# Attention into a two-stage MoE: value products with queries on partitions, row sums from a column of ones

## The chip, the cores and the metric

One Trainium2 chip; the kernel runs on one of its cores. A core has five instruction streams: PE (TensorE, matmuls, with its weight loads shown apart as PEld), DVE (VectorE), ACT (ScalarE), POOL (GpSimd) and SP (SyncE, which here only issues DMAs). Each stream runs its own instructions in the order in which they stand in the program and waits on semaphores for the others. The metric is the device time of one execution in microseconds (us), the median of several runs.

## The reference

Three stages follow each other. The first is an attention with local and global tokens (4 batches, 8 heads, 512 local and 32 global tokens, head size 64); the second a dense layer pair with a piecewise activation; the third a routed layer pair with eight experts. Only the first is touched here:

```python
k_all = concat([k_g, k_l]);  v_all = concat([v_g, v_l])        # 32 + 512 tokens
out_g = sm(scale * q_g @ k_all.T) @ v_all                      # every global query sees all 544
s_ll = where(abs(i - j) <= 32, scale * q_l @ k_l.T, -1e9)      # a local query sees a band of 65 ...
a_l = sm(concat([scale * q_l @ k_g.T, s_ll]))                  # ... and the 32 global tokens
out_l = a_l @ concat([v_g, v_l])
# sm(s): e = exp(s - max(s));  e / (sum(e) + 1e-9)
```

## The kernel before

The attention is cut into 8 units (4 batches, 2 groups of 4 heads). A unit has two head pairs (`hl` = 0, 1), and a head pair has two steps of 2 x 128 queries, so a unit has four steps `k` = 0 to 3. A step works on `i` = 0 to 3: two query tiles by two heads.

What a unit does, with the names of its tiles:

- `pair`, `tr_k`, `tr_q`: keys and queries of a head pair are copied side by side (`kp`, `qp`), transposed on PE into `pk`, `pq` and copied to `kw`, `qT`. `kw` holds for every 64 queries 64 local keys and the 32 global keys (a block of 96 columns), so that 160 columns from a block's start hold the 128 local keys of a window and the global ones, with the window cut in two. `kw_g` writes the global keys into the blocks.
- `scores` (L484): PE forms `s`, 160 scores for each query; DVE (L496) adds the mask and takes the row's extreme into `st`; ACT (L506) takes the exponential into `sm` and has the row sum added up on the way, which it reads out with an instruction of its own (ACTIVATION_READ_ACCUMULATOR).
- `fin`: DVE turns the sums into reciprocals (L523, L524), POOL multiplies the rows by them (`pn`, L528, four of them; `smg`, L532, the global columns).
- `trans`: PE transposes `pn` into `ta` (four) and `smg` into `tb`; ACT copies them to `ptA` and `ptB`.
- `pval`: PE forms the output transposed, head dimension on partitions, in `pv`: the values are the weights (`va`, `vb` for the two halves of a window, L580; `vgz` for the global tokens, L593), the probabilities stream through. `ptA` has 32 more columns for each tile, which hold the global queries' probabilities (`pglob`), so that the global output falls out of the same matmuls (and of two more, L586). ACT copies `pv` to `xs`; `gsum` sums the global part into `xg` and stores the local part to DRAM (`xsc`) from ACT's DMA queue.
- `glob_s` to `glob_t`: scores `sg` of the global queries (L424, L421), maximum, exponential with sums, division on POOL (L455), transposition into `pgT`.

Between these stand pieces that prepare the weights of the second stage (`conv_half` on DVE, `conv_parts` on ACT and POOL). Two pieces of the second stage's first matmul (`up1`, tile `hps`) are put into the attention's last unit; `act1`, `down1` (tile `yp`) follow.

The order of all this is written out by hand: every call gets a number from the table `AT` (a unit is 16 long, so unit `n` starts at 16 n; the names with `z_` are those of unit 0), the calls are sorted by it, and each engine's stream follows. PSUM, where matmuls write, is held in pools: `psh` with two buffers for `s` and `hps`, and `ps` with three buffers under the tag T (`ta`, `tb`, `sg`) and three under the tag y (`pk`, `pq`, `pgt`, `pv`).

Of the kernel before, what the change touches and what calls it, by code (L numbers as in the profile page):

```python
# [22 lines left out]
    scores=[-0.929, 3.577, 6.9, 12.21], fin=[6.425, 8.774, 10.199, 17.022],  # L23
    trans=[9.521, 10.799, 15.847, 20.797], pglob=[9.927, 14.287, 19.392, 22.324],
    pval=[13.081, 18.61, 24.832, 25.923], gsum=[27.805, 30.229], glob_s=1.311, glob_m=2.56, glob_e=3.521,
    glob_n=4.146, glob_p=6.373, glob_t=9.066, ld0=-3.002, ld1=-0.136, ld_v=18.09, ld_vb=15.197, ld_vg=16.913,
    k0=9.379, q0=10.782, k1=14.997, q1=14.811, u0=127.057, u1=141.542, rk0=3.621, rq0=4.32, rk1=9.51,
    rq1=11.797, e_k='V', e_q='V', e_g='P', bp=1, e_kc='A', e_kd='A', e_w='V', e_fl='P', e_qc='A', f4='PPPP',
    e_p='P', e_ta='A', e_tb='A', e_xs='A', e_pt='V', e_pu='V', gl=6.839, gt0=22.889, gt1=24.82,
    z_scores=[0.0, 1.0, 5.699, 12.227], z_fin=[2.374, 7.66, 10.375, 14.481],  # L30
    z_trans=[3.713, 13.16, 15.237, 21.686], z_pglob=[8.77, 15.092, 19.345, 23.598],
    z_pval=[14.413, 19.634, 23.697, 26.493], z_glob_s=2.772, z_glob_m=3.337, z_glob_e=3.472, z_glob_n=3.787,
    z_glob_p=5.475, z_glob_t=7.797, cl=[17.691, 30.997, 37.177, 47.387, 52.623, 67.27, 78.231, 90.2, 98.587],
    xh=[25.339, 28.196, 38.872, 43.513, 47.597, 59.508, 67.7, 73.729],
    xlo=[25.905, 33.595, 42.625, 46.625, 54.263, 70.623, 75.965, 79.01], cp=1.664,
)
CV = [1.668, 10.165, 12.547]
# [4 lines left out]
def kernel(  # L42
# [88 lines left out]
    ps = at_st.enter_context(tc.tile_pool(name="ps", bufs=3, space=PSUM))  # L131
# [3 lines left out]

    HP = P // 2
    NW = P + G
    BW = HP + G
# [149 lines left out]
    NH = 4  # L288
# [12 lines left out]
    def ld_va(n):  # L301
        u = units[n]
        u.va = ap_.tile([P, NH, NT, D], F32, name="va", tag="va", bufs=2)
        r0 = (u.b * H + NH * u.g) * S - W
        vat = u.va.rearrange("p h t d -> p (h t) d")
# [7 lines left out]
    def ld_vb(n):  # L313
        u = units[n]
        u.vb = ap_.tile([P, NH, NT, D], F32, name="vb", tag="vb", bufs=2)
        r0 = (u.b * H + NH * u.g) * S + W
        vbt = u.vb.rearrange("p h t d -> p (h t) d")
# [6 lines left out]
    def ld_vg(n):  # L324
# [3 lines left out]
        for j in range(2):  # L328
            for t in range(2):
                p0 = (2 * t + j) * G  # L330
                nc.sync.dma_start(
                    out=vz[p0 : p0 + G, :, t, j * D : (j + 1) * D],
                    in_=v_g[u.b, h0 : h0 + NH].rearrange("(l j) s d -> j s l d", j=2)[j],
                )
        nc.sync.dma_start(out=u.vb[HP + W :, :, NT - 1], in_=v_g[u.b, h0 : h0 + NH].rearrange("h s d -> s h d"))

    class Unit:
        def __init__(self, n):
# [5 lines left out]
            self.pn = {}  # L344
            self.xs = {}
            self.st = {}
            self.pt = {}
            self.ptA = {}
# [3 lines left out]
    NKW = 8 * BW + HP  # L352
# [14 lines left out]
    def tr_k(n, hl):  # L367
        u = units[n]
        pk = ps.tile([P, S], F32, name="pk", tag="y")
# [3 lines left out]
        copy(  # L373
            AT["e_kc"],
            kw[:, BW : 8 * BW].rearrange("p (c x) -> p c x", x=BW)[:, :, :HP].rearrange("p c (y t) -> p c y t", t=NT),
            pk.rearrange("p (t y) -> p y t", t=NT)[:, 8 : P - 8, :].rearrange("p (c y) t -> p c y t", c=7),
        )
        copy(
            AT["e_kd"],
            kw.rearrange("p (c x) -> p c x", x=W)[:, 1 : NKW // W - 1 : NKW // W - 3, :].rearrange(  # L380
                "p c (y t) -> p c y t", t=NT
            ),
            pk.rearrange("p (t y) -> p y t", t=NT).rearrange("p (c y) t -> p c y t", c=16)[:, 0:16:15],
        )
# [3 lines left out]
    def kw_g(n, hl):  # L388
# [5 lines left out]
            kw[:, : 8 * BW].rearrange("p (c x) -> p c x", x=BW)[:, :, HP:],  # L394
            kg.unsqueeze(1).to_broadcast([P, 8, G]),
# [3 lines left out]
            kw.rearrange("p (c x) -> p c x", x=W)[:, 0 : NKW // W : NKW // W - 1, :],  # L399
# [3 lines left out]
    def tr_q(n, hl):  # L403
        u = units[n]
        pq = ps.tile([P, S], F32, name="pq", tag="y")
# [5 lines left out]
    def glob_s(n):  # L411
        u = units[n]
        sg = ps.tile([P, 512], F32, name="sg", tag="T")
        sg2 = ps.tile([P, 512], F32, name="sg2", tag="y")
        for glob in range(2):
            for i in range(2):
                for j in range(2):
                    rs = slice((2 * i + j) * G, (2 * i + j + 1) * G)
                    lq = qgz[:, 2 * u.g + i, j, u.b * G : (u.b + 1) * G]
                    if glob:  # L420
                        nc.tensor.matmul(sg2[rs, :G], lhsT=lq, rhs=u.kw[i][:, HP:BW], start=True, stop=True)  # L421
                        continue
                    kl = u.kw[i][:, W : W + 8 * BW].rearrange("p (c y x) -> p c y x", c=8, x=W)[:, :, 0:3:2, :]
# [3 lines left out]
    def glob_m(n):  # L427
# [3 lines left out]
        nc.vector.tensor_reduce(out=m[:, 0:1], in_=sg, axis=AX.X, op=ALU.max)  # L431
        nc.vector.tensor_reduce(out=m[:, 1:2], in_=sg2[:, :G], axis=AX.X, op=ALU.max)
# [4 lines left out]
    def glob_e(n):  # L437
# [3 lines left out]
        pl, pr = pg[:, W : W + S], pg[:, W + S :]  # L441
        nc.scalar.activation(out=pl, in_=sg, func=AF.Exp, scale=scale, bias=m[:, 2:3], accum_out=m[:, 3:4])
        nc.scalar.activation(out=pr, in_=sg2[:, :G], func=AF.Exp, scale=scale, bias=m[:, 2:3], accum_out=m[:, 4:5])

    def glob_n(n):
        u = units[n]
        m = u.gm
        nc.vector.tensor_scalar(
            out=m[:, 5:6], in0=m[:, 3:4], scalar1=m[:, 4:5], scalar2=1e-9, op0=ALU.add, op1=ALU.add
        )  # L450
        nc.vector.reciprocal(out=m[:, 6:7], in_=m[:, 5:6])

    def glob_p(n):
        m = units[n].gm
        nc.gpsimd.tensor_scalar(  # L455
            out=pg[:, W:], in0=pg[:, W:], scalar1=m[:, 6:7], scalar2=1.0, op0=ALU.mult, op1=ALU.mult
        )

    def glob_t(n):
# [3 lines left out]
        pt = ps.tile([P, NT, P], F32, name="pgt", tag="y")  # L463
# [7 lines left out]

    def scores(n, k):
# [3 lines left out]
        st = u.st[k] = ap_.tile([P, 3, 4], F32, name="st", tag="st", bufs=4)  # L476
        sj = [psh.tile([P, 2, NW], F32, name=f"s{j}", tag="h") for j in range(2)]
        for tt in range(2):
            t = 2 * uu + tt
            for j in range(2):  # L480
                for c in range(2):
                    q0 = t * P + c * HP
                    k0 = (2 * t + c) * BW
# [7 lines left out]
        for j in range(2):  # L491
            for tt in range(2):
# [11 lines left out]
                    accum_out=st[:, 0, i : i + 1],  # L504
# [10 lines left out]
    def sel(x):  # L515

        ap = x[:, :HP]
        return bass.AP(ap.tensor, ap.offset, [list(ap.ap[0]), [BW, 2], [1, HP]])

    def fin(n, k):  # L520
        u = units[n]
        sm, st = u.sm.pop(k), u.st.pop(k)
        nc.vector.tensor_scalar(out=st[:, 2, :], in0=st[:, 1, :], scalar1=1e-9, scalar2=None, op0=ALU.add)  # L523
# [1104 lines left out]
```

## Time and profile before

| what | us |
|---|---|
| median of 3 runs (lowest, highest) | 747.02 (746.94, 748.74) |
| the profiled execution, its own time | 748.24 |
| its span in the trace | 746.5 |
| attention, until `yp` starts | 146.5 of it |

The profiled execution lies 1.22 us above the median of the runs. Its span is 1.74 us shorter than its device time; what lies around the span is not in the trace. A row of the timeline gives the start, the duration, the engine, the line, the operation and the tiles; where matmuls follow one another, the distance between two starts is the cost, since a matmul's shown end overlaps the next start. Matmuls stand twice in the trace when both operands are fp32 and it isn't a transposition: "x4" are then two matmuls of the program. The granted clock of TensorE was 1.00 of full speed in all of the attention.

### The profile page before, as it was taken

The page shows a single profiled execution, that of the slowest core. Times are in us where ns is not written, and L with a number is a line of the kernel's source. Part 1 is how long each engine was busy: PE and PEld are TensorE (multiplying, and loading weights), DVE is VectorE, ACT ScalarE, POOL GpSimd, SP SyncE. Part 2 cuts the span into 40 slices and gives each one's busy share as a digit, 9 for nine tenths or more (in the row PEclk, how much of TensorE's full clock was granted, in tenths as well). Part 3 has the DMA queues.
Part 4 walks back from the last instruction along what each step waited for, and adds up shares of the span by engine and source line. Part 5 has one row for each costly group of instructions (what it writes and reads, how often), then busy time and mean ns, then how long its engine had stood idle before and what let it go on. Part 6 is the DMA issues. An engine that isn't in the chain of part 4 may idle for free.

```text
span 746.5 us, 14099 instructions
## 1 busy us (share of the span) xinstructions
PE 734.2 (98%) x4999; PEld 592.5 (79%) x4999; DVE 480.7 (64%) x1473; ACT 372.2 (50%) x929; POOL 138.2 (19%) x301
## 2 busy tenths in 40 slices
PE   8999999999999999999999999999999999999996
PEld 6776776788888888888898888888888876777774
DVE  4899997388888757777698866785788322211111
ACT  4899998655455565455556646555312212211111
POOL 4676776312111100000000100000003002001011
PEclk9999999999999999999999999999999999999999
DMA  8678884423343612000200032212301466557560
GB/s 191 161 196 219 227 207 123 115 86 114 113 124 103 225 58 72 0 1 1 98 1 1 1 98 71 72 35 93 100 0 57 148 230 226 179 192 269 174 228 25
DMA packets 83067, 86.45 MB, mean 116 GB/s; under 512 B 42816, under 2 KB 57152, under 8 KB 82992
## 3 DMA queue, kind: packets, MB, share of 16 engines
q1 hardware_dynamic: 75760, 77.64, 34.9%
q0 software_dynamic: 1648, 4.98, 1.7%
q10 hardware_dynamic: 5584, 2.88, 1.4%
q8 instruction: 41, 0.67, 0.4%
q14 instruction: 34, 0.28, 0.1%
HBM read 73.93 MB, written 11.94 MB: 115 GB/s over the span
## 4 chain that ended last, share of the span: by engine, by line
PE 77%; issue 13%; DMA 4%; DVE 2%; ACT 2%; POOL 2%; POOLq 0%; ACTq 0%
PE yp L881 25%; PE hps L832 25%; PE eh L1359 7%; PE eo L1381 6%; DMA out<-ob,ide 3%; PE s L484 3%; PE pv L580 3%; PE pv L593 2%; PE ta L552 1%; POOL out L1393 1%; PE wt L1471 1%; PE sg L424 1%; PE pq L407 1%; DVE sm L496 1%; PE pk L371 1%
## 5 line engine op out<-in xcount | busy, mean ns | idle before, releaser
L832 PE MATMUL hps<-xh,winh 128*128 128x512 f32 (+2 forms) x320 | 115.0, 359 | 0.0
L832 PE MATMUL hps<-xl,winh 128*128 128x512 f32 (+2 forms) x320 | 114.4, 358 | 0.0
L832 PE MATMUL hps<-xh,winl 128*128 128x512 f32 (+2 forms) x320 | 114.3, 357 | 0.0
L881 PE MATMUL yp<-woh,gh 128*128 128x512 f32 x272 | 107.5, 395 | 0.4 <-ACT gh L850 0.4
L881 PE MATMUL yp<-wol,gh 128*128 128x512 f32 x272 | 106.3, 391 | 0.0
L1365 DVE SCALAR_TENSOR_TENSOR el<-eh,eg 128x512 fp32r<-128x512 f32 (+2 forms) x40 | 24.4, 611 | 100.1 <-ACT eg L1364 99.8
L1364 ACT ACTIVATE eg<-eh 128x512 fp32r<-128x512 f32 (+2 forms) x40 | 21.4, 535 | 105.9 <-PE eh L1359 102.6
L832 PEld LDWEIGHTS hps<-xh,winh 128*128 128x128 f32 x320 | 60.3, 188 | 9.0 <-PE pv L593 0.2
L832 PEld LDWEIGHTS hps<-xh,winl 128*128 128x128 f32 x320 | 60.3, 188 | 8.5
L832 PEld LDWEIGHTS hps<-xl,winh 128*128 128x128 f32 x320 | 60.2, 188 | 7.6
L1393 POOL DMA_INDIRECT out<-ob,ide x17 | 17.1, 1006 | 249.3 <-DVE ob L1390 245.7
L1359 PE MATMUL eh<-exh,wh 128*128 128x512 f32 (+2 forms) x160 | 59.6, 372 | 0.0
L881 PEld LDWEIGHTS yp<-woh,gh 128*128 128x128 f32 x272 | 51.1, 188 | 10.2 <-ACT gh L850 0.8
L881 PEld LDWEIGHTS yp<-wol,gh 128*128 128x128 f32 x272 | 51.2, 188 | 9.4
L1359 PE MATMUL eh<-exl,wh 128*128 128x512 f32 (+2 forms) x160 | 57.3, 358 | 1.0 <-PEq L1569 1.0
L1359 PE MATMUL eh<-exh,wl 128*128 128x512 f32 (+2 forms) x160 | 57.2, 358 | 0.0
L506 ACT ACTIVATE sm<-sm,st 128x160 f32<-128x160 f32 x128 | 53.4, 427 | 4.9 <-DVE st L496 4.9
L1381 PE MATMUL eo<-wh,eg 128*128 128x512 f32 x136 | 53.3, 392 | 0.0
L1381 PE MATMUL eo<-wh,el 128*128 128x512 f32 x136 | 53.1, 391 | 0.0
L1381 PE MATMUL eo<-wl,eg 128*128 128x512 f32 x136 | 53.1, 391 | 0.0
L528 POOL TENSOR_SCALAR pn<-sm,st 128x128 f32<-128x128 f32 x128 | 50.7, 416 | 9.0 <-DVE st L524 4.4
L865 DVE TENSOR_TENSOR wol<-wof,woh 128x512 fp32r<-128x512 f32 x64 | 43.9, 686 | 0.0
(808 smaller groups left out, 1590.6 us busy)
## 6 DMA issues: line engine op xcount, KB each, us to landing
rw<-in_moe_w SPq DMA_DIRECT2D x64, 256.0 KB, 4.4
rw<-in_moe_w SPq DMA_DIRECT2D x24, 512.0 KB, 4.8
raw<-in_moe_w_out SPq DMA_DIRECT2D x12, 512.0 KB, 3.7
raw<-in_moe_w_in SPq DMA_DIRECT2D x11, 512.0 KB, 3.7
k<-in_k_l SPq DMA_DIRECT2D x16, 256.0 KB, 3.0
ysc<-y SPq DMA_DIRECT2D x16, 256.0 KB, 2.1
ye<-ysc SPq DMA_DIRECT2D x16, 256.0 KB, 2.8
q<-in_q_l SPq DMA_DIRECT2D x15, 256.0 KB, 4.1
```

The lines of the kernel that those rows point to most:

```text
L484: nc.tensor.matmul(sj[j][c * HP : (c + 1) * HP, tt, :], lhsT=u.qT[hl][j * D : (j + 1) * D, q0 : q0 + HP], rhs=u.kw[hl][j * D : (j + 1) * D ...
L506: nc.scalar.activation(out=sm[:, i, :], in_=sm[:, i, :], func=AF.Exp, scale=-1.0, bias=st[:, 0, i : i + 1], accum_out=st[:, 1, i : i + 1],)
L528: eng_of[AT["f4"][i]].tensor_scalar(out=pn[:, i, :].rearrange("p (c x) -> p c x", c=2), in0=sel(sm[:, i, :]), scalar1=st[:, 2, i : i + 1], ...
L580: nc.tensor.matmul(pv[j * D : (j + 1) * D, tt, c0:c1], lhsT=v[:, 2 * hl + j, t, :], rhs=ptA[:, 2 * tt + j, c0:c1], start=tt == 0 and c0 == ...
L832: nc.tensor.matmul(hp_[:, :n], lhsT=wt[:, kk, fs], rhs=xt, start=kk == 0 and i == 0, stop=kk == KD - 1 and i == 2)
L865: nc.vector.tensor_tensor(out=wol, in0=wof[f // 2][:, f % 2, :], in1=woh.bitcast(F32), op=ALU.subtract)
L881: nc.tensor.matmul(B_.yp[i], lhsT=gt[:, cs], rhs=wt, start=f == 0 and k == 0, stop=f == KF - 1 and k == 2)
L1359: nc.tensor.matmul(hps[:, :n], lhsT=w[:, fs], rhs=x, start=kk == 0 and i == 0, stop=kk == KD - 1 and i == 2)
L1364: nc.scalar.activation(out=gh, in_=hps[:, :n], func=AF.Relu)
L1365: nc.vector.scalar_tensor_tensor(out=gl, in0=hps[:, :n], scalar=0.0, in1=gh.bitcast(F32), op0=ALU.max, op1=ALU.subtract)
L1381: nc.tensor.matmul(B_.yp[i], lhsT=a[:, cs], rhs=w, start=f == 0 and k == 0, stop=f == KF2 - 1 and k == 2)
L1393: nc.gpsimd.indirect_dma_start(out=outs[t], out_offset=bass.IndirectOffsetOnAxis(ap=ide[:, t : t + 1], axis=0), in_=ob, in_offset=None, bo ...
```

## The change

The value product is turned over. The probabilities (exponentials, not divided) become the weights, the values stream through, and the output has queries on partitions. The values get a 65th column of ones, so that the row sum stands beside the output; DVE divides when it reads `pv`, the result `xq` is transposed back on PE (`px`), and ACT copies that to `xs`. The global queries' product gets matmuls of its own (`og`), is divided and transposed likewise (`on`, `ot`). `kw` holds for every 64 queries its whole window of 128 keys and then the 32 global ones (1280 columns in place of 832). All tiles of `ps` share one ring of six buffers.

```diff
-    ps = at_st.enter_context(tc.tile_pool(name="ps", bufs=3, space=PSUM))
+    ps = at_st.enter_context(tc.tile_pool(name="ps", bufs=6, space=PSUM))
+    D1 = D + 1
+    vas, vbs, vgz = (
+        [ap_.tile([P, n, D1], F32, name=f"{x}{i}", bufs=1) for i in range(2)]
+        for x, n in (("va", NH * NT), ("vb", NH * NT), ("vgz", 2 * 4))
+    )
+    for t in vas + vbs:
+        nc.gpsimd.memset(t[:, :, D:], 1.0)
...
-    NKW = 8 * BW + HP
+    NKW = NWIN * NW
...
+        keys(AT["e_kc"], NW, NW, NWIN - 2, W // NT, HP // NT, P // NT)
+        keys(AT["e_kd"], W, (NWIN - 1) * NW - W, 2, 0, (S - P + W) // NT, (P - W) // NT)
...
-        nc.scalar.activation(out=pl, in_=sg, func=AF.Exp, scale=scale, bias=m[:, 2:3], accum_out=m[:, 3:4])
+        nc.scalar.activation(out=pl, in_=sg[:, W:], func=AF.Exp, scale=scale, bias=m[:, 2:3])
...
-    def glob_n(n):
-    def glob_p(n):
+    def glob_v(n):
+        u = units[n]
+        u.og = og = ps.tile([P, 512], F32, name="og", tag="T")
+        for t in range(NT + 1):
+            for h in range(NH):
+                hs = slice(h * G, (h + 1) * G)
+                l, r = (u.pgT[:, t, hs], u.va[:, h, t]) if t < NT else (pgBs[n % 2][:, hs], u.vb[:, h, NT - 1])
+                nc.tensor.matmul(og[hs, :D1], lhsT=l, rhs=r, start=t == 0, stop=t == NT)
+    def glob_f(n):
+        nc.vector.tensor_scalar(out=m[:, 3:4], in0=u.og[:, D:D1], scalar1=1e-9, scalar2=None, op0=ALU.add)
+        nc.vector.reciprocal(out=m[:, 4:5], in_=m[:, 3:4])
+        u.on = ap_.tile([P, 2, D], F32, name="on", tag="on")
...
+    def glob_x(n):
+        nc.tensor.transpose(ot[:, :P], u.on.rearrange("p j d -> p (j d)"), ident)
...
                 nc.scalar.activation(
                     out=sm[:, i, :],
                     in_=sm[:, i, :],
                     func=AF.Exp,
                     scale=-1.0,
-                    bias=st[:, 0, i : i + 1],
-                    accum_out=st[:, 1, i : i + 1],
+                    bias=st[:, i : i + 1],
                 )
-    def fin(n, k):
...
+    def gcol(n, k):
         u = units[n]
+        copy(AT["e_g"], sg, u.sm[k][:, :, P:])
...
         for i in range(4):
-            nc.tensor.transpose(ta[:, i, :], pn[:, i, :], ident)
+            nc.tensor.transpose(ta[:, i, :], sm[:, i, :P], ident)
...
-    def pglob(n, k):
...
     def pval(n, k):
+        pv = ps.tile([P, 4, D1], F32, name="pv", tag="T")
+        for i in range(4):
+            tt, j = divmod(i, 2)
+            for c, v in enumerate((u.va, u.vb)):
+                cs = slice(c * HP, (c + 1) * HP)
+                nc.tensor.matmul(
+                    pv[cs, i], lhsT=ptA[:, i, cs], rhs=v[:, 2 * hl + j, 2 * uu + tt], start=i == 0, stop=False
+                )
+        nc.tensor.matmul(
+            pv.rearrange("p i d -> p (i d)"), lhsT=ptB, rhs=u.vz[:, 4 * hl : 4 * hl + 4].rearrange("p i d -> p (i d)"),
+            start=False, stop=True,
+        )
+        nc.vector.tensor_scalar(out=sr[:, 0], in0=pv[:, :, D], scalar1=1e-9, scalar2=None, op0=ALU.add)
+        nc.vector.reciprocal(out=sr[:, 1], in_=sr[:, 0])
+        nc.vector.tensor_tensor(
+            out=u.xq[hl][:, 2 * uu : 2 * uu + 2].rearrange("p t (j d) -> p (t j) d", j=2), in0=pv[:, :, :D],
+            in1=sr[:, 1].unsqueeze(2).to_broadcast([P, 4, D]), op=ALU.mult,
+        )
+    def xtr(n, hl):
+        for t in range(NT):
+            nc.tensor.transpose(px[:, t, :], u.xq[hl][:, t, :], ident)
+        xs = u.xs[hl] = ap_.tile([P, NT, P], F32, name="xs", tag="xs")
+        copy(AT["e_xs"], xs, px)
```

The table `AT` has new numbers throughout, of which a reader learns little; two places of it name engines, and these move work: the copies `kp`, `qp` go from DVE to POOL, those of the global keys into `kw` and of `pgT` from DVE to ACT:

```diff
-    rq1=11.797, e_k='V', e_q='V', e_g='P', bp=1, e_kc='A', e_kd='A', e_w='V', e_fl='P', e_qc='A', f4='PPPP',
+    u1=134.478, rk0=3.915, rq0=7.329, rk1=9.43, rq1=9.988, e_k='P', e_q='P', bp=1, e_kc='A', e_kd='A', e_w='A',
```

How the order moves is shown at three places. The first is PE in the middle of a unit, where two blocks of scores (`s`, numbers are buffers) follow each other closely; before:

```order
L484 MATMUL s_1686<-kw,qT 64x160 x2
L552 MATMUL ta<-ident,pn 128x128 x4
L553 MATMUL tb<-ident,smg 128x128
L484 MATMUL s_1735<-kw,qT 64x160 x2
L484 MATMUL s_1736<-kw,qT 64x160 x2
```

and after, at the same place:

```order
L509 MATMUL s_1426<-kw,qT 64x160 x2
L589 MATMUL px<-ident,xq 128x128 x4
L459 MATMUL pgt<-ident,pg 128x128 x4
L463 MATMUL pgt_1464<-ident,pg 128x128
L509 MATMUL s_1469<-kw,qT 64x160 x2
```

Between the two blocks of scores stood one step's transpositions of probabilities; now it is the transpositions back and those of the global probabilities.

The second is PE at the end of a value product; before:

```order
L580 MATMUL pv<-ptA,vb 64x64 x2
L586 MATMUL pv<-pgB_156,vb 64x32 x2
L593 MATMUL pv<-ptB,vgz_150 64x128 x4
L407 MATMUL pq<-ident,qp 128x128 x4
L552 MATMUL ta<-ident,pn 128x128 x4
```

and after:

```order
L570 MATMUL pv<-vb_152,ptA 64x65
L573 MATMUL pv<-vgz_154,ptB 128x260
L554 MATMUL ta<-ident,sm 128x128 x4
L555 MATMUL tb<-ident,smg 128x128
L378 MATMUL pk<-ident,kp 128x128 x4
```

One matmul over all 128 queries and 260 columns stands where four of 64 by 128 stood.

The third is ACT at the end of the attention, where `xs` and its DMA are the last before the second stage's first activation (`hps,half`); before:

```order
L357 COPY xs<-pv 128x320
L357 COPY ptA<-ta 128x4x128
L357 COPY ptB<-tb 128x128
L357 COPY xs<-pv 128x320 x2
L605 DMA xsc<-xs 128x4x128 x2
L846 ACTIVATE t__3000<-hps,half 128x512
```

and after:

```order
L364 COPY xg<-ot 64x2x32 x2
L364 COPY ptA<-ta 128x512
L364 COPY ptB<-tb 128x128
L364 COPY xs<-px 128x512
L595 DMA xsc<-xs 128x512
L835 ACTIVATE t__3016<-hps,half 128x512
```

Two copies and two DMAs stood there, now it is one of each, and what it copies comes from a transposition of `xq`.

## Rows read from the trace of the kernel before

**Rows 1.** Busy time of each engine in three stretches, by windows.

```profile
core 0: us, PE busy (x) PEld busy (x) DVE busy (x) ACT busy (x) POOL busy (x), PEclk, DMA share, GB/s
...
60.00:92.00 32.00, 31.49 (x470) 23.27 (x468) 30.27 (x137) 30.73 (x119) 24.26 (x59) 1.00 0.83 214
...
124.00:146.00 22.00, 21.83 (x291) 17.61 (x286) 9.86 (x48) 15.59 (x54) 11.44 (x30) 1.00 0.42 112
146.00:746.50 600.50, 593.64 (x3044) 486.33 (x3043) 368.66 (x960) 250.21 (x475) 42.13 (x46) 1.00 0.30 99
```

**Rows 2.** Timeline of PE, three places: start, duration, engine, line, operation.

```profile
28.36 0.78 PE L484 MATMUL s<-kw,qT 64*64 64x160 f32 x16
29.06 0.39 PE L580 MATMUL pv<-ptA,va 128*64 128x96 f32 x4
29.28 0.28 PE L580 MATMUL pv<-ptA,vb 128*64 128x64 f32 x4
29.39 0.34 PE L580 MATMUL pv<-ptA,va 128*64 128x96 f32 x4
...
29.68 0.26 PE L586 MATMUL pv<-pgB,vb 128*64 128x32 f32 x4
29.76 0.64 PE L593 MATMUL pv<-ptB,vgz 128*64 128x128 f32 x8
30.33 0.66 PE L552 MATMUL ta<-ident,pn 128*128 128x128 f32 x4
30.82 0.27 PE L553 MATMUL tb<-ident,smg 128*128 128x128 f32 x1
30.93 0.60 PE L179 MATMUL pgl<-ident,gl 128*128 128x128 f32 x4
...
42.19 1.46 PE L424 MATMUL sg<-kw,qgz 128*32 128x512 f32 x8
43.07 0.64 PE L421 MATMUL sg<-kw,qgz 128*32 128x32 f32 x8
43.64 0.39 PE L580 MATMUL pv<-ptA,va 128*64 128x96 f32 x4
...
139.97 0.61 PE L593 MATMUL pv<-ptB,vgz 128*64 128x128 f32 x8
140.41 0.34 PE L580 MATMUL pv<-ptA,va 128*64 128x96 f32 x4
```

**Rows 3.** Chain that ended last: first and last of seven `sg` blocks.

```profile
27.77 0.60 PE sg L424 x2
...
122.91 0.60 PE sg L424 x2
```

**Rows 4.** Timeline of PE, where it waits inside a unit.

```profile
61.69 0.74 PE L552 MATMUL ta<-ident,pn 128*128 128x128 f32 x4
...
62.72 1.21 PE L484 MATMUL s<-kw,qT 64*64 64x160 f32 x16
63.87 0.39 PE L580 MATMUL pv<-ptA,va 128*64 128x96 f32 x4
```

**Rows 5.** Timeline of ACT: reading out a row sum, and copies.

```profile
59.34 0.18 ACT L506 ACTIVATION_READ_ACCUMULATOR sm<-sm,st 128x1 f32 x1
59.44 0.41 ACT L506 ACTIVATE sm<-sm,st 128x160 f32<-128x160 f32 x1
...
67.36 0.64 ACT L357 COPY kw<-pk 128x448 f32<-128x448 f32 x2
67.89 0.59 ACT L357 COPY ptA<-ta 128x512 f32<-128x512 f32 x1
```

**Rows 6.** Chain that ended last, at 116 us and where the second stage starts.

```profile
116.02 4.67 DMA xsc<-xs
...
142.27 1.33 ACTq L605
...
146.48 2.62 PE yp L881 x9
```

More of the change, by code (lines that the diff above doesn't have):

```diff
@@ L29 @@
[L29 to L34, printed above, removed]
@@ L368, in tr_k @@
         u = units[n]
-        pk = ps.tile([P, S], F32, name="pk", tag="y")
+        pk = ps.tile([P, S], F32, name="pk", tag="T")
         for t in range(NT):
@@ L372, in tr_k, with keys @@
         kw = u.kw[hl] = ap_.tile([P, NKW], F32, name="kw", tag="kw")
[L373 to L384, printed above, removed]
+        kv, pkv = kw[:, :], pk[:, :]
+        part = [list(x.ap[0]) for x in (kv, pkv)]
+        def keys(e, at, step, m, y0, dy, ny):
+            copy(
+                e,
+                bass.AP(kv.tensor, kv.offset + at, [part[0], [step, m], [NT, ny], [1, NT]]),
+                bass.AP(pkv.tensor, pkv.offset + y0, [part[1], [dy, m], [1, ny], [P, NT]]),
+            )
+        keys(AT["e_kc"], NW, NW, NWIN - 2, W // NT, HP // NT, P // NT)
+        keys(AT["e_kd"], W, (NWIN - 1) * NW - W, 2, 0, (S - P + W) // NT, (P - W) // NT)
         if n or hl:
@@ L462, in glob_t @@
             warm(32)
-        pt = ps.tile([P, NT, P], F32, name="pgt", tag="y")
+        pt = ps.tile([P, NT, P], F32, name="pgt", tag="T")
         for c in range(NT):
@@ L572, in pval @@
         if uu == 0:
-            u.xs[hl] = ap_.tile([P, NT, G + P], F32, name="xs", tag="xs", bufs=2)
-        pv = ps.tile([P, 2, G + P], F32, name="pv", tag="y")
-        for tt in range(2):
-            t = 2 * uu + tt
-            end = t == NT - 1
-            for v, c0, c1 in ((u.va, 0, G + HP), (u.vb, G + HP, G + P)):
-                for j in range(2):
-                    nc.tensor.matmul(
-                        pv[j * D : (j + 1) * D, tt, c0:c1], lhsT=v[:, 2 * hl + j, t, :], rhs=ptA[:, 2 * tt + j, c0:c1],
-                        start=tt == 0 and c0 == 0, stop=False,
-                    )
-            if end:
-                for j in range(2):
-                    nc.tensor.matmul(
-                        pv[j * D : (j + 1) * D, tt, :G], lhsT=u.vb[:, 2 * hl + j, t, :],
-                        rhs=pgBs[n % 2][:, (2 * hl + j) * G : (2 * hl + j + 1) * G], start=False, stop=False,
-                    )
@@ L590, in pval @@
-        for tt in range(2):
-            for j in range(2):
-                js = slice(j * D, (j + 1) * D)
-                nc.tensor.matmul(pv[js, tt, G:], lhsT=u.vz[:, hl, tt, js], rhs=ptB, start=False, stop=tt == 1)
-        copy(AT["e_xs"], u.xs[hl][:, 2 * uu : 2 * uu + 2, :], pv)
-    def gsum(n, k):
-        u = units[n]
-        nc.vector.tensor_reduce(
-            out=xg[:, 2 * u.g + k // 2, u.b * G : (u.b + 1) * G], in_=u.xs[k // 2][:, :, :G].rearrange("p t q -> p q t"),
-            axis=AX.X, op=ALU.add,
-        )
-        hp = 2 * u.g + k // 2
+            u.xq[hl] = ap_.tile([P, NT, P], F32, name="xq", tag="xq", bufs=1)
```

151 lines of the change are left out of this document (68 added, 83 removed).

## The prediction

> **What bounds the kernel now.** I read the windows first, then PE's timeline in one unit, then the chain of waits. From 146 us on PE is busy 593.6 of 600.5 us, and nothing there is in the diff [rows 1]; only the 146.5 us before it can change. In the middle of the attention four engines are close to full: in 32 us PE is busy 31.5, ACT 30.7, DVE 30.3, POOL 24.3 us, at the full clock (1.00) [rows 1]. PE's busy time contains overlapping ends, so I take its need from the distances between starts [rows 2]: a block of scores 0.70 us (28.36 to 29.06), one step's transpositions 0.60 (30.33 to 30.93), a value product 1.27 (29.06 to 30.33), or 1.19 without its two matmuls on `pgB` (0.08, 29.68 to 29.76), so 1.23 on average, four transpositions 0.49 (30.33 to 30.82), the global scores 1.45 (42.19 to 43.64). A unit needs 4 x 0.70 + 4 x 0.60 + 4 x 1.23 + 4 x 0.49 (`pk`, `pq`) + 5 x 0.12 (`pgt`) + 1.45 = 14.1 us. It lasts 15.86 us: 95.14 us for six units [rows 3]. So PE works 89% of a unit and stands about 1.6 us in it (the rest is two extra sets of transpositions in one of the units). The reader is to see two of those waits in [rows 4]: `ta` and `tb` take 1.03 us (61.69 to 62.72) where 0.60 are needed, and the scores behind them 1.15 (62.72 to 63.87) where 0.70 are. The first waits for POOL's `pn`, the second for a free buffer of `s`, which DVE must have read. No engine alone is the bound; each has little slack, and the queues' coupling costs the last tenth.
>
> **PE: what a unit gains and loses.** (a) Value product. Eight matmuls of 64 by 65 columns: two of 64 columns take 0.11 us (29.28 to 29.39 [rows 2]), so 8 x 0.056 = 0.45. The matmul for the global tokens, 128 by 260, has no row of its own. From below, four transpositions of the same width take 0.49, so 260 columns 0.25; from above, four half-width products of 128 columns take 0.44 (139.97 to 140.41 [rows 2]), 0.11 each, twice that at full width, so 0.45. I take 0.45, since it is a product and no transposition. Going from 64-wide to full-width work costs 0.13: L593 takes 0.57 before transpositions (29.76 to 30.33) and 0.44 before more 64-wide work [rows 2]. In all 1.03 for 1.23: -0.2 in each of four steps, -0.8. The Trainium skill (TensorEngine Tiling (Array Packing), Key Properties) says that changing the tiling mode, not just the tile, drains the engine. That speaks against this change: by the two orders I count 16 changes of mode in a unit where there were 14, 2 x 0.13 us more; the 0.13 is what the trace has for such a drain, and by that rule alone the eight units would lose 2 us.
>
> (b) `px`: two blocks of four transpositions, 2 x 0.49, +0.98. (c) `og`: 20 matmuls 32 wide by 65 columns. From below: four of 512 columns take 0.88 (42.19 to 43.07), so 0.028 for 65. From above: four of 32 columns take 0.57 with the wait in it (43.07 to 43.64), 0.14 each. The nearest row has two of 32 columns in 0.08 (L586), 0.04 each. I take 0.035: +0.7, between 0.56 and 2.8. (d) `ot` is one more transposition and the second global block has 64 columns for 32: +0.15. Sum: -0.8 + 0.98 + 0.7 + 0.15 = +1.0 us a unit. PE then needs 15.1 us of the 15.86.
>
> **The other engines.** ACT loses 18 read-outs of a sum at 0.10 each (59.34 to 59.44 [rows 5]): -1.8. Its key copies grow from 512 columns in 0.53 (67.36 to 67.89 [rows 5]) to 960, +0.47 for each of two; the global keys (256 columns, 0.27 each by the same row) come from DVE, +0.55; `pgT` too, 512 columns, +0.5; `xs` shrinks from four copies of 320 to two of 512, -0.3; `ot` brings +0.2. The sum is +0.1: ACT stays as full as it is. DVE gives up `kp`, `qp`, `pgT`, the global keys and the sums over `xs`, and takes a division of 256 columns in each step; POOL gives up `pn`, the scaling of `pg` and the copies into `ptA`, and takes `kp`, `qp`. Both get slack, which costs and gives nothing by itself.
>
> **Waits.** `ta` now reads `sm` itself, so the 0.43 for `pn` goes. Between the two close blocks of scores stand 0.49 + 0.6 us of transpositions in place of 0.60, so most of the 0.45 behind them goes. The wait of the `xs` copy for its own DMA (4.67 us in the chain at 116 us [rows 6]) goes, since the buffer is written a whole unit later. What is late next: the keys, since ACT's path from `pk` to `kw` gets 2 x 0.5 us longer and `sg` waits for it; `px`, which waits for DVE's division of the last step; and the ring of six PSUM buffers. Behind a waiting `px` all of PE's queue stands, the scores first. I let half of the wait stay, 0.85 of 1.6 us; the bounds are 0.2 (only the keys) and 1.7 (as now). A unit: +1.0 - 0.75 = +0.25 to +0.3; seven units +2.0.
>
> **Both ends.** In unit 0 the added PE work stands beside the shorter way from exponential to transposition and beside 32 filler matmuls that stay: 0, give or take 1. At the end, now: the last copy (0.4) and two DMA issues (1.33 [rows 6]) before the second stage's first activation. Then: the division (three DVE operations; three of ACT's 0.41 [rows 5] would be 1.2, and I estimate 0.85, since two of the three have four columns), `px` 0.49, a copy of 0.59 [rows 5] and one issue, half of 1.33: 2.6 for 1.75, +0.85, of which PE covers a little with `hps`: +0.7.
>
> **Sum.** +2.0 + 0 + 0.7 = +2.7. Against the profiled execution that is 748.24 + 2.7 = 750.9; it lies 1.22 above the median, so a median of 747.02 + 2.7 = 749.7.
>
> **Rivals.** Faster: PE's waits nearly vanish. For it: both waits of [rows 4] have their cause removed and two engines get slack; against it: ACT is as full as before and feeds PE in every step. With 0.2 us of wait a unit and the global-token matmul at 0.35, a unit changes by +0.6 - 1.4 = -0.8; seven of them and the end: -4.9, 742.1. It decides as soon as less than 0.5 us of wait is left in a unit at my price of PE's work. No change: ACT sets the pace, with 96% busy [rows 1] and work that stays the same within 0.1 us; a unit remains at 15.8 and PE's added work fills its holes: +0.7 for the end, 747.7. Slower still: 24 tiles a unit go through six PSUM buffers, 4.0 us for each (6 / 24 x 15.86), where 10 and 10 went through three and three, 4.8 us each; `sg` and `og`, which wait for two engines, hold up the tiles behind them, and the waits stay as long as now. Then +1.0 x 7 + 0.7 = +7.7, 754.7.
>
> **How the numbers follow.** The forecast has 0.45 (its own range 746 to 753), faster 0.22, no change 0.20, slower still 0.13. A measurement of this kernel tells about 0.3%, 2.2 us, from no change. Of the forecast's 0.45 some 0.32 lie above 749.3, the rest within; of no change, 0.16 lie within and 0.04 under it. Slower: 0.32 + 0.13 = 0.45; same 0.13 + 0.16 = 0.29; faster 0.22 + 0.04 = 0.26. The range for 8 in 10 reaches from just above the faster rival to just beyond the slowest, 743 to 756: the price of `og` alone could add 2 us a unit at its upper bound, which I leave outside.
>
> **What would show it.** The step of 8 + 1 matmuls: 1.03 us from `pv` to `ta`. The block of 20: 0.7. Distance of `sg` blocks: 15.9 to 16.4 us for the forecast, about 15.1 for the faster rival, 16.9 for the slow one. `ta` behind `s` at 0.60 without a wait for POOL. `yp` starts at 149 us of the span instead of 146.5. The forecast is wrong if the `sg` distance falls under 15.7, or if L573 costs 0.25 rather than 0.45, for then PE needs only 14.3.

## The result, and the profile after

The changed kernel takes 756.78 us (median; 755.8 to 760.56), the kernel before 746.99 in the same runs: ratio 1.0127, interval 1.0109 to 1.0146, that is 9.8 us slower where 2.7 were forecast. The profiled execution took 757.61 us with a span of 755.9. The second stage is as it was; all of the loss lies before it. The windows answer to [rows 1] (columns as there):

```profile
60.00:92.00 32.00, 28.96 (x444) 22.07 (x446) 23.05 (x110) 27.52 (x77) 6.78 (x17) 1.00 0.76 202
...
156.00:755.90 599.90, 593.90 (x3047) 486.70 (x3045) 368.68 (x960) 249.89 (x475) 42.05 (x46) 1.00 0.30 99
```

From 156 us on PE is busy 593.90 us, where it was 593.64 [rows 1]. In the middle of the attention every engine is *less* busy than before: PE 28.96 of 32 for 31.5, ACT 27.5 for 30.7, DVE 23.1 for 30.3. DVE and POOL also gave up work; PE's work grew. That is what longer waits look like, and by itself it says nothing about which engine causes them.

PE's timeline, answering to [rows 2] and [rows 3]: a value product with what follows it, the global product, and `sg` of the second and the last unit.

```profile
23.04 0.71 PE L573 MATMUL pv<-vgz,ptB 128*128 128x260 f32 x2
23.67 0.67 PE L473 MATMUL og<-va,pgT 128*32 128x65 f32 x32
24.16 0.29 PE L473 MATMUL og<-vb,pgB 128*32 128x65 f32 x8
24.39 0.77 PE L509 MATMUL s<-kw,qT 64*64 64x160 f32 x16
25.09 0.27 PE L570 MATMUL pv<-va,ptA 128*64 128x65 f32 x1
...
25.70 0.71 PE L573 MATMUL pv<-vgz,ptB 128*128 128x260 f32 x2
26.25 0.60 PE L554 MATMUL ta<-ident,sm 128*128 128x128 f32 x4
...
30.70 1.07 PE L432 MATMUL sg<-kw,qgz 128*32 128x512 f32 x8
31.58 0.29 PE L429 MATMUL sg<-kw,qgz 128*32 128x64 f32 x8
31.81 0.27 PE L570 MATMUL pv<-va,ptA 128*64 128x65 f32 x1
...
131.50 1.06 PE L432 MATMUL sg<-kw,qgz 128*32 128x512 f32 x8
```

The eight matmuls take 0.61 (25.09 to 25.70), the global one 0.55 before transpositions (25.70 to 26.25) and 0.63 before 32-wide work (23.04 to 23.67): 1.16 to 1.24 a step. `og` takes 0.72 (23.67 to 24.39), `sg` 1.11 (30.70 to 31.81) where it took 1.45 [rows 2]. Six units take 131.50 - 30.70 = 100.8 us, 16.80 each, for 15.86 [rows 3]. The 15.86 goes by the last matmuls of a `sg` block, which in the kernel before wait inside the block; after, the two ways of counting give the same. By the first matmul of a block (26.18 and 120.18) the unit before took 15.67. So a unit grew by 0.94 to 1.13 us, by the mark that is taken; I go on with 0.94.

From the third unit on, PE now stands once a unit at a value product, 0.9 to 1.6 us from the fourth on. First that place on PE, then the same time on ACT:

```profile
114.16 0.60 PE L554 MATMUL ta<-ident,sm 128*128 128x128 f32 x4
...
116.52 0.70 PE L573 MATMUL pv<-vgz,ptB 128*128 128x260 f32 x2
118.15 0.27 PE L570 MATMUL pv<-va,ptA 128*64 128x65 f32 x1 [0.93 <-ACT ptA L364]
```

```profile
113.43 1.04 ACT L364 COPY kw<-pk 128x768 f32<-128x768 f32 x2
114.50 0.40 ACT L364 COPY kw<-kgT 128x256 f32<-128x256 f32 x1
114.81 0.58 ACT L364 COPY xs<-px 128x512 f32<-128x512 f32 x1
115.42 0.33 ACTq L595 DMA_DIRECT2D xsc<-xs  x1
115.79 1.38 ACT L531 ACTIVATE sm<-sm,st 128x160 f32<-128x160 f32 x4 [0.40 <-DVE wof L232]
117.08 0.41 ACT L364 COPY xg<-ot 64x64 f32<-64x64 f32 x2
117.51 0.58 ACT L364 COPY ptA<-ta 128x512 f32<-128x512 f32 x1
```

`ta` is written by 114.8, but ACT copies it only at 117.51. In front of that copy stand the longer key copies (1.04), the global keys (0.40), `xs` with its DMA issue, four exponentials and the two copies `xg`, and only the exponentials and `xs` are not new or longer. The 0.40 in brackets is in truth the DMA issue of 115.42. The read-outs of [rows 5] are gone: four exponentials are one run of 1.38 us.

The end, from the chain that ended last, answering to [rows 6]:

```profile
149.88 0.69 PE pv L570 x16
150.57 0.65 PE pv L573 x2
...
151.65 0.44 DVE xq L580
...
152.13 0.44 PE px L589 x2
152.57 4.18 PE hps L821 x24
156.75 2.92 PE yp L870 x12
```

The wait for `xsc` is gone, as forecast. The first `yp` matmul starts at 156.58 (the chain's row, 156.75, begins later), 10.1 us after before's 146.48. Of that, 0.8 is the start (scores at 9.44 for 8.66), which is not the change's doing (run `d4` below), 5.7 six units, and 3.7 the first and the last unit: 2.6 from the first `sg` to the end of the second (13.3 to 15.9 us), 1.0 from the end of the last `sg` to `yp` (23.6 to 24.6).

### The profile page after: what moved, and what is told of

The parts are those of the page before. It is cut to its first block, busy times and chain, and to the rows that moved or that the text cites. A ratio compares the mean times of both kernels' runs of the same rounds, so it can differ in the third digit from the quotient of the medians.

```text
span 755.9 us, 14037 instructions
## 1 busy us (share of the span) xinstructions
PE 738.8 (98%) x5135; PEld 599.9 (79%) x5135; DVE 471.5 (62%) x1446; ACT 374.8 (50%) x808; POOL 85.4 (11%) x173
## 4 chain that ended last, share of the span: by engine, by line
PE 77%; issue 13%; DMA 3%; ACT 3%; DVE 2%; POOL 2%; POOLq 0%; ACTq 0%
PE yp L870 25%; PE hps L821 25%; PE eh L1348 7%; PE eo L1370 6%; PE s L509 3%; DMA out<-ob,ide 3%; PE pv L570 2%; PE pv L573 2%; PE ta L554 1%; ACT sm L531 1%; POOL out L1382 1%; PE wt L1460 1%; PE px L589 1%; PE pk L378 1%; PE pq L414 1%
## 5 line engine op out<-in xcount | busy, mean ns | idle before, releaser
L531 ACT ACTIVATE sm<-sm,st 128x160 f32<-128x160 f32 x128 | 44.3, 420 | 10.4 <-DVE st L521 8.4
L521 DVE CUSTOM_DVE_ANT_0 sm<-s,mask 128x160 f32<-128x160 f32 x128 | 33.8, 321 | 14.7 <-PE s L509 14.5
```

The source lines that it names most:

```text
L521: nc.vector.tensor_tensor_reduce(out=sm[:, i, :], in0=sj[j][:, tt, :], in1=mask[:, mi, :], scale=-scale, scalar=3.0e38, op0=ALU.add, op1=A ...
L531: nc.scalar.activation(out=sm[:, i, :], in_=sm[:, i, :], func=AF.Exp, scale=-1.0, bias=st[:, i : i + 1],)
```

## The experiments

Attention below means from the first `sg` to the first `yp` in the trace: 132.0 us before (14.47 to 146.48), 141.4 after (15.23 to 156.58). It is read from one trace each; how far that can be trusted is shown by the kernel before, which has 132.0, and 132.6 with one ring (further below), at the same total. Ratios are to the kernel before; the changed kernel has 1.0127.

**Less work on ACT.** Two engine choices back to DVE: `e_w='A'` to `'V'` and `e_pt='A'` to `'V'`.

> The changed kernel, but the columns of the global keys (e_w) and the copy of pgt (e_pt) go back from ACT to DVE, where they were before: ACT loses 2 x 0.31 + 0.48 = 1.1 us a unit, PE's queue and all else is the same. Theory A (ACT's queue, in which the exponentials stand behind longer copies, makes the second value product of each unit wait for ptA): that wait, 0.94 us at 118.15 and 134.87, shrinks by more than half, a unit falls from 16.8 to 16.2 or less, 752 to 753 us. Theory B (PE's own added work makes the time): 756 to 758, as the changed kernel's 756.8. Theory C (DVE, blocked in order on the value products, is what is late): 758 or more, since DVE gets 1.1 us more.

770.33 us, ratio 1.0300 (1.0286 to 1.0314), attention 157.4. Waits of DVE in 46 to 131 us (in total, times, longest):

```profile
DVE kw L364 <- ACT kw L364: 16.5, 9, 2.1
DVE sm L521 <- PE s L509: 3.0, 4, 1.5
```

DVE now stands in order behind ACT's key copies, and the masks behind it. The relief turned into a wait, and TensorE's clock fell (last section), so the run doesn't tell the theories apart. Each half alone:

```
a6:  e_pt='A' -> 'V'                  (pgT on DVE)
a7:  e_w='A'  -> 'P'                  (global keys on POOL)
c1:  both
c2:  both, and  nc.scalar.dma_start(out=xsc...) -> nc.sync.dma_start
c4:  c2, and the order of a8 (below)
```

> The changed kernel with only the copy of pgt (e_pt) back on DVE; the columns of the global keys stay on ACT. The run with both moved took 770.3, and its trace has DVE waiting 16.5 us for ACT's key copies in front of its own. Theory A (ACT's queue is late, and that wait was what spoilt the relief): 752 to 756. Theory C (anything more in DVE's queue delays the masks): 758 or more.

755.76, ratio 1.0097 (1.0079 to 1.0115).

> The changed kernel with the columns of the global keys (e_w) copied by POOL instead of ACT, so ACT has 2 x 0.31 us less a unit and DVE nothing more. POOL stands behind the ACT copy of the same tile, and has 10 of 32 us busy. Theory A: ptA and kw come 0.3 to 0.6 us earlier, 753 to 756 us. Theory B (PE) or C (DVE): 756 to 758. If POOL's slower copy makes the scores or sg wait for keys: 758 or more.

756.69, ratio 1.0102 (1.0081 to 1.0123).

> The changed kernel with the copy of pgt on DVE and the columns of the global keys on POOL (the two moves that gave 0.3% and 0.25% less of the ratio to before when made alone): ACT 0.48 + 0.62 = 1.1 us less a unit. Theory A2: the two add up, 7 x 0.6 to 1.1 less, 749 to 753. Theory B: 755 to 757.

755.12, ratio 1.0084 (1.0065 to 1.0103), attention 138.6. Each alone is at the edge of what can be told; the two together are some 3 us better than the changed kernel, where 4 to 8 were expected. The sign of the theory holds, its size doesn't. In the trace the wait for `ptA` shrinks by more than the time does: in the eight units from 6.4 us to 1.6. Part of it comes back elsewhere, as 1.0 of PE's wait for a load of `va`, 0.4 for POOL's `qp` (0.1 before), and 0.3 in the first unit for POOL's copies into `kw`.

> As the kernel before this one (pgt on DVE, global keys on POOL), and the DMA of xs into xsc is issued by SP's queue instead of ACT's: two issues of 0.37 us and the wait in front of each leave ACT's queue in the units from the third on, some 0.5 to 0.6 us a unit. Theory A2: another 2 to 3 us less, 747 to 750. Theory B: no difference. If SP's queue, in which the loads of the next unit stand behind the wait for xs, holds up loads: longer than the kernel before this one.

754.51, ratio 1.0079 (1.0060 to 1.0097): no further gain that can be told. In the profiled execution the clock fell (0.50 in 88 to 90 us) and a load of values came late in SP's queue in one unit (a row of its chain), so this run is no clean test of the move:

```profile
98.40 6.59 DMA va<-in_v_l
```

> As the kernel before this one (three moves off ACT), with the fourth value product and its px one place later, as in the run that did only that. If ACT's lateness at this place is gone with its work, nothing is gained: within 1 us of the kernel before this one. If PE still stands there for ptA: 1 to 3 us less.

754.84, ratio 1.0083 (1.0066 to 1.0100): nothing gained.

**More work on ACT.**

```
  scalar.activation(out=sm[:, i, :], ..., bias=st[:, i : i + 1],
+                   accum_out=st[:, 4 + i : 5 + i])
```

> The changed kernel with one thing taken back that the change removed: each of the 16 exponentials of a unit reads out its sum again (accum_out into four more columns of st, which nothing uses). ACT gets 16 x 0.092 = 1.47 us a unit, nothing else changes. ACT's own work, each operation at its shortest distance to the next, is 15.1 us of a unit of 16.8, as 14.3 was of 15.7 before. Theory A2 (ACT's work sets the unit, which is some 10% longer than it): 7 x 1.5 to 1.6 more, 766 to 768. Theory B (PE's work sets it, ACT has 1.7 us of slack): 757 to 760.

768.18, ratio 1.0256 (1.0236 to 1.0277), attention 152.0, 10.6 longer. PE's wait for `ptA` in 46 to 131 us grows; first the changed kernel, then this one:

```profile
PE pv L570 <- ACT ptA L364: 5.1, 4, 1.6
```

```profile
PE pv L571 <- ACT ptA L364: 7.9, 5, 1.9
```

So 8 x 1.47 = 11.8 us put on ACT cost 10.6, but not evenly and not all by ACT. The first two units (to the third `sg`) cost 0.1; the other six and the end cost 10.5 for 8.8 put on. Up to 1.7 of that is TensorE's clock, which fell in this run at 88 to 94 us, to 0.50 at the lowest (last section). So ACT has room in the first two units and none from the third on, although it is busy only 27.5 of 32 us there. It isn't simply full either: in the fourth to seventh unit of the changed kernel ACT itself waits 0.3 to 0.9 us for PE's `ta`. To see its real load I took, for each kind of ACT instruction, the short distance (15th percentile) to the next start, and summed that over the six units: 14.3 to 14.6 us a unit before, by where the units are cut, 15.1 after. By kind: key copies 1.06 to 2.11, global keys 0 to 0.62, `pgT` 0 to 0.48, `xg` 0 to 0.40, `xs` 1.17 to 0.93, read-outs 1.65 to 0; the DMA issues of `xsc` are 12 in both kernels.

**Less work on PE.** `og` without 16 of its 20 matmuls (with `start` set to fit):

```
- for t in range(NT + 1):
+ for t in range(NT, NT + 1):
```

> The changed kernel; left out are 16 of the 20 matmuls of og in each unit (only those on pgB stay, so the global queries' output is not the reference's). Everything else, the copy of pgT too, stays. It takes 16 x 0.035 = 0.56 us of PE's time out of a unit. Theory B (PE's own work sets the pace): 756.8 - 8 x 0.56 = 752.3. Theory A (PE waits for ACT later in the unit anyway): 755.5 to 757, since the wait grows by what PE saves.

The total of 1328.21 us can't be read: the tokens' routing in the second stage follows from the values. Attention is 141.0, 0.3 shorter, for 4.5 us of work removed by the estimate (3.7 by the rows: the `og` that is left takes 0.25 for 0.71). PE alone isn't the limit. Then the two by two table, with half of each global-token matmul left out too:

```
- nc.tensor.matmul(pv.rearrange(...), lhsT=ptB, rhs=u.vz[:, 4*hl : 4*hl+4]...
+ nc.tensor.matmul(pv.rearrange(...)[:, :2*D1], lhsT=ptB, rhs=u.vz[:, 4*hl : 4*hl+2]...
d2: the same, with e_pt='V', e_w='P'
```

> The changed kernel; left out are 16 of the 20 matmuls of og in each unit and the second half (130 of 260 columns) of each matmul for the global tokens, so the attention's result is not the reference's and only the time up to the first yp may be read. PE has 0.56 + 4 x 0.25 = 1.56 us less in each of eight units, 12.5 in all; ACT and DVE keep their work. Theory AB (PE and ACT are both close to their limits, so that relieving one alone gives little): the distance from the first sg to the first yp falls from 141.4 by 1 to 4 us. Theory B (PE's work alone): by 9 to 12.

> As the kernel before this one, and with ACT's copy of pgt on DVE and its copies of the global keys on POOL (together 1.1 us of ACT less a unit, which alone brought that distance from 141.4 to 138.6). Theory AB: the two reliefs together give more than the sum of each alone, the distance falls to 128 to 134. If latency or DVE's order is the limit and neither engine: it stays at 136 to 138.6.

Their totals (1341.31 and 1336.21) can't be read either. Attention (one profile each):

```
                      ACT as it is    ACT 1.1 us a unit less
PE as it is               141.4              138.6
PE 1.56 us a unit less    139.5              134.2
```

By the rows the 1.56 is rather 1.33: `og` 0.46 less and the halved matmul some 0.22 less, four times. Two rows of the run with less work on PE:

```profile
116.28 0.49 PE L573 MATMUL pv<-vgz,ptB 128*128 128x130 f32 x2
116.60 0.60 PE L554 MATMUL ta<-ident,sm 128*128 128x128 f32 x4
```

Each relief alone gives 1.9 and 2.8, both 7.2. That would be the pattern of two engines that are both at the edge, but the 139.5 holds a fall of the clock (0.50 in 64 to 66 us, last section), worth up to 1.5 us; without it the two alone come to as much as 6.2. What stands firmer is where the time goes, in us:

```
                                   first two units   the other six, to yp
kernel before                            27.7               104.3
changed kernel                           31.0               110.3
more work on ACT                         31.2               120.8
ACT 1.1 us a unit less                   31.6               107.0
PE 1.56 us a unit less                   29.1               110.4
both less                                30.1               104.1
```

In the first two units PE's work sets the time: less of it gains 1.9, more on ACT costs 0.1. In the other six it is ACT first: less on PE alone gains nothing there (up to 1.5 with the clock's loss added back), less on ACT 3.3, both 6.2, which is the time of the kernel before. Still, 134.2 is just outside the range expected, and what remains of the loss lies in the first two units.

**DVE, the ring, the order, the start.** CV put back to `[1.668, 10.165, 12.547]`; two of three conversion operations left out; two rings (`bufs=6` to 3, and `tag="y"` for `pk, pq, sg2, pgt, og, pv, px`; `ot` stayed in the first); and, in the kernel before, one ring (`bufs=3` to 6, every `"y"` to `"T"`).

> The changed kernel with the three places in a unit at which DVE converts weights put back to those of the kernel before (CV 1.668, 10.165, 12.547 instead of 0.284, 9.4, 15.94). Theory C (DVE's order delays the masks, and by them exponentials and ptA): 752 to 755 us. Theories A (ACT's queue) and B (PE's work): within 1.5 of 756.8.

758.28, ratio 1.0144 (1.0128 to 1.0159): no gain.

> The changed kernel; of the three DVE operations of each weight conversion the second and third are left out (the weights of the second stage are not the reference's, so only the attention, up to the first yp at 156.6 us, may be read). DVE gets 0.87 us less at each of three places a unit, 2.6 us of its 11.5. Theory C (DVE's queue delays masks, maxima and divisions): attention ends 4 to 8 us earlier. Theories A and B: within 1.5 us of 156.6.

Attention 141.9 (after 141.4). DVE's work isn't the limit.

> The changed kernel with its one ring of six PSUM buffers split again into two of three: sg, ta, tb and pgt2 in one, pk, pq, sg2, pgt, og, pv and px in the other. If the common ring is what holds tiles up (the rival called slower still), the time falls by 2 us or more, to 754 or less. If not, it stays at 756.8 or rises, because three buffers are fewer for pv and px, which wait for DVE: 757 to 760.

773.99, ratio 1.0354 (1.0339 to 1.0368). The clock fell here as well (0.57 in 66 to 70 us, and four times more), so not all of the 17 us are the ring's. PE's weight loads in 46 to 131 us:

```profile
PEld sg L432 <- ACT xg L364: 14.4, 5, 3.1
```

Three tiles ahead of `sg` stands `ot`, and its buffer is free only after ACT's `xg`. The common ring keeps this wait away; another split in two was not tried.

> The kernel before with one part of the change alone: its two rings of three PSUM buffers become one of six. In the changed kernel the opposite step, two rings of three, cost 17 us, so the rival that blamed the common ring had the sign wrong. If the ring helps any order of tiles: 743 to 746. If the order of the kernel before is fitted to its two rings: 746 to 749. If tiles that wait for two engines (sg) hold up the others in a common ring: 749 or more.

747.74 for 747.61, ratio 1.0001 (0.9992 to 1.0010). The ring by itself is worth nothing in the old order. With the run before it, the rival that blamed it falls.

```
a8: pval 4th 19.3 -> 20.1, xtr 2nd 20.634 -> 21.4
```

> The changed kernel with one place moved: the fourth value product of a unit (pval 19.3 to 20.1) goes behind the next unit's first transpositions and second scores, and its transposition px (20.634 to 21.4) behind it. No work and no engine is changed. Theory A (PE stands at this product about 0.94 us a unit because ACT's copy of ta comes 3.3 us after ta): PE fills the wait with those 1.3 us of work, 7 x 0.5 to 0.9 less: 750 to 753.5. Theory B (PE's work): 756 to 757.5. Theory C (DVE, blocked in order): 757 or more, as DVE's division then stands behind the next masks or ahead of them just as blocked.

756.40, ratio 1.0109 (1.0089 to 1.0129). The wait of `pv` for `ptA` leaves PE's list for 46 to 131 us, and this takes its place:

```profile
PE px L589 <- DVE xq L580: 3.5, 5, 0.7
```

```
d4: the first pair's second key copy: e_kd 'A' -> 'V'
```

> The changed kernel with the second key copy of the first head pair alone (2 x 96 columns) on DVE beside ACT's first. If the start's 0.8 us (scores at 9.44 instead of 8.66) is the longer chain of key copies on ACT, the first scores start at 9.0 to 9.2 and the first yp 0.2 to 0.4 us earlier. If DVE's copies of the global keys, which took 1.38 us there for 0.40, are the cause: no change or later.

756.47, one run, which can't show 1 us; so by the traces:

```profile
9.44 0.77 PE L509 MATMUL s<-kw,qT 64*64 64x160 f32 x16 [1.33 <-DVE kw L364]
```

```profile
8.14 0.77 PE L509 MATMUL s<-kw,qT 64*64 64x160 f32 x16 [0.72 <-DVE kw L364]
```

The first row is the changed kernel's first scores, the second this one's: 1.3 earlier, far more than expected. But versions whose start is the changed kernel's differ as much among themselves; `a8` has

```profile
7.86 0.78 PE L509 MATMUL s<-kw,qT 64*64 64x160 f32 x16 [0.40 <-ACT qT L364]
```

From `pk` to the first scores it is 3.3 us in the changed kernel's trace, but 2.24 to 2.40 in twelve other versions with that same start, 2.57 in the kernel before and 2.23 in it with one ring; here it is 2.63. In the five traces in which it is 3.3 to 3.5, DVE's two copies of the global keys take 1.16 to 1.38 us, in the twelve 0.39 to 0.56; the changed kernel's:

```profile
7.91 1.38 DVE L364 COPY kw<-kgT 128x256 f32<-128x256 f32 x2 [0.40 <-ACT kw L364]
```

So the start's 0.8 is one execution's, not the price of the longer key copies on ACT, and this run moved nothing that can be told. Why those two DVE copies are slow in some executions was not tried.

Last, the order alone: `trans` 8.2, 12.6, 16.3, 20.2; `pval` 12.7, 17.0, 21.0, 24.7; `xtr` 18.5, 26.8 (and the first unit's and `xh`, `xlo` some 2 to 5 later).

> The changed kernel with every engine's work kept and only the order moved: each step's transpositions go behind the next scores but one order place later (trans 8.2, 12.6, 16.3, 20.2 for 3.8, 8.4, 13.5, 17.0), its value product and px 4 to 5 later still (pval 12.7, 17.0, 21.0, 24.7), so that scores and value product of a step lie 12.5 to 13.3 places apart instead of 6.9 to 10.9; before it was 13.7 to 17.9. Theory L (too little distance between the stages of a step, so each wait on ACT and DVE shows on PE): waits of 1.3 us a unit fall by half or more, 749 to 753. Theory AB (PE and ACT full, distance does not matter): 755 to 758. If the end, where nothing fills the longer distance, costs more than the units gain: above 757.

756.34, ratio 1.0109 (1.0090 to 1.0128), attention 141.3. The chain through one unit:

```profile
111.42 1.00 PE sg L432 x8
112.42 0.11 PE sg L429 x8
112.53 0.59 PE px L589 x4
113.12 0.70 PE s L509 x16
113.83 0.59 PE ta L554 x4
...
115.14 0.64 PE pv L573 x2
...
126.80 0.64 PE pv L573 x2
127.43 0.98 PE sg L432 x5
```

No other engine and no wait stands in it, in the pieces left out as well. PE works without a pause, and a unit still takes 127.43 - 111.42 = 16.0 us: more than the 15.86 of the kernel before with its waits. The order buys this with dearer blocks: `ta` behind scores 0.59 for 0.44 behind a full-width product, the global product 0.64 for 0.55. I count 20 changes of tile width in this unit, and 14 in the changed kernel's from 114.8 to 131.5. The units between take 17.3 to 17.6: in two of them PE stands 1.2 us at a `px`, by the profile 0.9 for ACT's `ptA` and 0.3 for DVE's `xq`. The last `sg` to `yp` takes 27.3 for 25.1.

> The same order, and ACT without the copy of pgt (DVE) and the columns of the global keys (POOL), which alone gave 1.7 to 3 us. Theory L: the two gains add up or more, 746 to 750, level with the kernel before. Theory AB: 753 to 756, as with the two moves alone.

758.22, ratio 1.0130 (1.0110 to 1.0151): no gain from ACT in this order. Theory L holds for the waits of every other unit, and fails for the time.

## Why the prediction was wrong

The direction was right, the size was not: +2.7 forecast, +9.8 measured. Three terms of the sum failed: PE's need and the wait that stays, about equally, in each unit, and the first unit, put at nothing.

- **PE's need, step (a).** I priced the value product at 1.03, with one change of width in it. It is 1.16 to 1.24, no cheaper than the old 1.23. The eight matmuls came as forecast (0.61 with the change of width, 0.58 forecast); the matmul of 260 columns takes 0.55 to 0.63, more even than the 0.45 that I had as its bound from above. Half of its columns take 0.32 (116.28 to 116.60 above), so 0.43 to 0.46 of it goes with the columns, as I had it, and some 0.1 doesn't: about what the traces have for a change of width, of which a step has two. `px` 0.49 and `og` 0.72 came as forecast. `sg` fell by 0.34, which I had as +0.15 with `ot`; but of the 1.45 some 0.25 was a wait that I took for need. In a later unit of the kernel before it is 1.20 (73.95 to 75.15, rows at the end). The sum of the blocks is 15.4 us in the changed order: +1.3 a unit for +1.0 (+1.5 if that wait is taken out of the old sum), and 16.0 in the order without waits. So the rival called faster (742) had a unit 0.8 shorter, and that could not be had: without any wait a unit of the changed order takes 15.4, 0.5 less than before (its second unit, in which the trace lists no wait of PE, took 15.56).
- **ACT, "the sum is +0.1".** It is +0.6 to +0.8. The copies were near (2.11 + 0.62 for 2.00 + 0.55); too small were the two `xg` copies (0.40 for 0.2), too large the gain from the read-outs (1.65 for 1.8) and from `xs` (0.24 for 0.3). In the six later units, where ACT had no room, this took what the removed waits gave. "I let half of the wait stay": of 1.75 us 1.4 stayed, not 0.85. `ta` no longer waits for POOL, as forecast, but its copy waits in ACT's queue, and a value product for that. That ACT's work sets this wait is shown by the run with more on ACT (8.8 to 10.5 us in those six units for 8.8 put on) and, with half the effect, by the reliefs (3.3 us there for 6.6 taken away).
- **The unit:** +1.3 - 0.35 = +0.95 where I had +0.25 to +0.3; measured 16.80 - 15.86 = 0.94, or 1.13 by the other mark. The agreement is no independent test, since the 1.4 of wait is the unit less the sum of its blocks.
- **The ends.** "In unit 0 the added PE work stands beside" other ways, "0, give or take 1": the first unit lost 2.6. PE's work sets the time there, as the run with less of it shows. The start's 0.8 came on top by chance and isn't the change's. From the end of the last `sg` on it was 1.0, where 0.7 and a part of a unit's 0.3 were forecast: near, though `px` waits 0.7 there for its division.
- **"Slower still"** came near in size (754.7, sg distance 16.9) for the wrong reason: a ring of six is neutral in the old order, and the new one does worse with two rings of three.

The Trainium skill (TensorEngine Tiling (Array Packing), Key Properties) says that a change of tiling mode drains the engine. The traces agree: 0.09 to 0.15 us a change here (0.64 against 0.55, 0.59 against 0.44). Nothing else rests on it.

What stays open: why the reliefs of ACT gave half in the six later units of what the load cost there, what part of the first two units' 3.3 us is the order and not PE's work, and how much of the table above a second trace of each kernel would change. No version run beats the kernel before; the best of the changed order is 754.5.

## What to carry to other kernels

Sum each engine's work by the distance from one start to the next, queue issues and small copies included, before calling an exchange even: with ACT's work at 14.4 of 15.9 us, 0.6 to 0.8 us more of it in a loop turned into a wait elsewhere. When two engines are both near the edge, relieving either shows little; test them together, and test by adding work, which shows at once. Read such runs unit by unit: PE set the time in the first two units and ACT in the other six, and the total shows neither. Look at the granted clock of each run before taking its difference for an engine's. And a bound for a new instruction that is put together from rows without the change of width around it is no bound.

## What the runs showed of the hardware

Busy time hides ACT's load: it was busy 27.5 of 32 us in 60 to 92 us, and the unit that lies in there (the fourth) grew by 1.5 us when 1.47 were put on ACT. TensorE's clock fell after PE had stood. In the run with DVE behind ACT's key copies, in the one with more work on ACT, and in the one with less on PE (two rows each; columns: window, length, PE, PEld, DVE, ACT, POOL busy, granted clock, DMA share, GB/s):

```profile
88.00:90.00 2.00, 0.24 (x2) 0.00 (x0) 1.90 (x8) 1.95 (x7) 1.09 (x2) 1.00 1.13 276
92.00:94.00 2.00, 2.00 (x21) 1.20 (x20) 0.50 (x2) 0.76 (x2) 0.00 (x0) 0.50 1.05 235
...
86.00:88.00 2.00, 0.08 (x3) 0.07 (x4) 0.67 (x3) 1.95 (x10) 0.85 (x2) 1.00 1.12 297
90.00:92.00 2.00, 2.00 (x20) 1.19 (x20) 0.42 (x1) 0.76 (x2) 0.00 (x0) 0.50 1.02 323
...
62.00:64.00 2.00, 0.95 (x16) 0.86 (x16) 0.13 (x1) 1.98 (x6) 0.45 (x1) 0.80 0.99 256
64.00:66.00 2.00, 2.00 (x13) 1.64 (x15) 0.77 (x3) 0.52 (x3) 0.82 (x2) 0.50 0.63 205
```

In the first, PE was all but idle from 88 to 90 us, and from 92 to 94 the granted clock was 0.50, 1.2 GHz. In the changed kernel, with waits of 0.9 to 1.6 us, it stayed at 1.00. So the 770 us of the first run, the 768 of the second and the 139.5 of the third hold a second loss behind the one that was meant to be measured. By the clock of the windows around these, taken as time lost by PE, it is up to 1.7 us in the second run and 1.5 in the third (an estimate).

And `sg`, whose columns of keys became four runs of 128 instead of pieces of 32, takes 0.88 us for its 512 columns either way (42.19 to 43.07 [rows 2], 30.70 to 31.58): the runs gave nothing. What shrank is the second part, 0.57 to 0.23 us although its matmuls have 64 columns for 32; the 0.57 holds a wait, and in another unit of the kernel before that part took 0.31 (74.84 to 75.15):

```profile
73.95 1.20 PE L424 MATMUL sg<-kw,qgz 128*32 128x512 f32 x8
74.84 0.38 PE L421 MATMUL sg<-kw,qgz 128*32 128x32 f32 x8
75.15 0.39 PE L580 MATMUL pv<-ptA,va 128*64 128x96 f32 x4
```
